# Weights converted from double by shift and masks, their exponents checked on ScalarE, with fewer conversion pieces in the attention

## The chip, the cores and the metric

The kernel runs on one core of one Trainium2 chip. The time is the device time of one execution in microseconds, as the median of three runs. The core has five engines that work in parallel, each in the order of its own program: TensorE (PE; its weight loads are shown as PEld), VectorE (DVE), ScalarE (ACT), GpSimd (POOL) and SyncE (SP), which issues nearly all DMAs here. TensorE has two clock levels, 1.2 and 2.4 GHz; the profile gives the granted clock as a share of the upper one, so 0.50 is 1.2 GHz and 1.00 is 2.4 GHz.

## The reference

The network has three parts, one behind the other. `moe_w_in`, `moe_w_out`, `moe2_w_ch1` and `moe2_w_ch2` come in as 64 bit doubles; all else is float32.

```python
# linear attention, B=4, H=8, S=768, D=48
for t in range(S):
    state = alpha[t][:, None] * state + outer(k[t], v[t])
    y[t] = q[t] @ state
# gating block: x is y with heads side by side, 768 x 384 per batch entry
h = gelu(x @ w_in)                      # w_in 384 x 1024
u, v = h[..., :512], h[..., 512:]
v = (v - mean(v)) / sqrt(var(v) + 1e-6) * g_ln
x = x + (u * (w_sg @ v + b_sg)) @ w_out # w_sg 768 x 768, w_out 512 x 384
# spectral mixing and MLP
u = x + real(fft2(x))
out = u + relu(norm(u) @ w_ch1) @ w_ch2 # w_ch1 384 x 1536, w_ch2 1536 x 384
```

## The kernel before

The order of the instructions of every engine is the order of the program text; nothing is rearranged by a scheduler. The kernel first runs the attention, then the gating block for the four batch entries, then the mixing and the MLP. Most matrix products are done three times, on a high and a low part of either operand, so weights and activations are split into `h` and `l` tiles.

**Attention.** There are 16 groups of two heads. Two scans per group on VectorE (L96, L114) form the decays, the product L115 the scaled keys, and GpSimd the scaled queries `qh` (L128). The loop runs over 32 half groups `h`, here called steps. In a step TensorE forms the scores of the next step (`sc`, L159), VectorE masks them (`att`, L164), TensorE transposes keys (`trk`, L134), ScalarE copies them to `kt` (L136), TensorE multiplies them with the values to `kp` (L146 and L147), VectorE scans `kp` into the state `z` (L151), and TensorE forms the output `y` (`pv`, L172, L173, L178), which ScalarE copies to `ys`. Scans for a group are issued two groups ahead; q and k are loaded five groups ahead.

**Weights.** The four double matrices are converted to float32 on the chip by the class `Wide`, in 62 blocks of 128 rows and 256 or 192 columns: 12 blocks of `w_in`, 8 of `w_out` (192 columns), 42 of the two MLP matrices, which are written back to memory (`w_s`) for later. A block is loaded raw as 16 bit words two blocks ahead. `first` takes exponent and upper mantissa bits out of the high word (`x`) and starts on the lower bits (`mid`); `second` sets the sign, forms the scale in `sb` and adds both parts on GpSimd (L468). In between, ScalarE changes the exponent's offset with an activation of `x` (L446, or L453). Up to the end of the attention (`on_dve`) VectorE forms `mid` with L448 and L465; later ScalarE and GpSimd do it with L451, L452, L454 and L467. Then `done` splits the result for `w_in` and `w_out` (ScalarE L392, GpSimd L395) or stores it.

`steps` is a generator that yields after each piece. While `on_dve` holds, a block is five pieces with one VectorE instruction each; later it is three pieces. Other code pulls pieces with `take`: in the attention `fill(h)` takes

```python
            if h == -1:
                take(wide, 1)
            if h >= 1:
                take(wide, 6 if h > 26 else 2)
```

`fill(29)` is called in step 30, behind the last `att`. In the gating block `gfill` takes one piece after each of the first 14 activations of a batch entry and 3 or 4 after each of the eight products with `w_sg`; `wo_ready` forces the blocks of `w_out` that the first batch entry needs.

**End.** `flag` sums up checks of the attention's scans at step 29 into `odd` (L313, L315, L316). At the end all engines load `odd` (L1167) and branch (L1168) round a general path, `attention_any` with a second `network`, which runs only where `odd` is set.

Of the kernel before, what the change touches and what calls it, by code (L numbers as in the profile page):

```python
# [317 lines left out]

def attention_any(tc, st):
# [106 lines left out]
class Wide:  # L426
    def __init__(self, nc, pool, w, const, ahead, on_dve):
        self.nc, self.pool, self.w, self.const, self.ahead, self.on_dve = nc, pool, w, const, ahead, on_dve
        self.n_done = 0
# [4 lines left out]
    def load(self, job):  # L434
        src, w, done = job
        raw = self.pool.tile([128, 4 * self.w], U16, tag="wr", name="wr", bufs=self.ahead + 2)[:, 0:4 * w]
        self.nc.sync.dma_start(raw, src)
        return dict(raw=raw, w=w, done=done, on_dve=self.on_dve, hi=raw.bitcast(I32).rearrange("p (a b) -> p a b", b=2)[:, :, 1])

    def first(self, j):  # L440
        nc, w = self.nc, j["w"]
        h16 = j["raw"].rearrange("p (a b) -> p a b", b=4)
        x, mid = j["x"], j["mid"] = self.tile("wx", I32, w, 2), self.tile("wm", F32, w, 3)
        nc.vector.tensor_scalar(out=x, in0=j["hi"], scalar1=0x7FFF0000, scalar2=None, op0=ALU.bitwise_and)
        if j["on_dve"]:
            nc.scalar.activation(x, x, AF.Relu, scale=8.0, bias=self.const)  # L446
            yield
            nc.vector.scalar_tensor_tensor(out=mid, in0=h16[:, :, 2], scalar=65536.0, in1=h16[:, :, 1], op0=ALU.mult, op1=ALU.add)  # L448
        else:
            low = j["raw"].bitcast(F32).rearrange("p (a b) -> p a b", b=2)[:, :, 0]  # L450
            nc.scalar.activation(mid, h16[:, :, 2], AF.Copy, scale=2.0 ** -20)  # L451
            nc.scalar.activation(low, h16[:, :, 1], AF.Copy, scale=2.0 ** -36)  # L452
            nc.scalar.activation(x, x, AF.Relu, scale=8.0, bias=self.const)  # L453
            nc.gpsimd.tensor_tensor(out=mid, in0=mid, in1=low, op=ALU.add)  # L454
        yield

    def second(self, j):
        nc, x, mid = self.nc, j["x"], j["mid"]
        sb = j["raw"].bitcast(I32).rearrange("p (a b) -> p a b", b=2)[:, :, 0]
# [11 lines left out]
    def steps(self, jobs):  # L471
        live = {i: self.load(jobs[i]) for i in range(self.ahead)}
        yield
        for i in range(len(jobs) + 2):
            if i - 1 in live:
                yield from self.second(live[i - 1])
            if i in live:
                yield from self.first(live[i])
# [33 lines left out]
def rows(ap, i, c, wide):  # L512
    if wide:
        ap, c = ap.bitcast(U16), slice(4 * c.start, 4 * c.stop)
    return ap[i * 128:(i + 1) * 128, c]


WJ = 256


def cols(n):
# [679 lines left out]
```

## Time and profile before

| | |
|---|---|
| median of 3 runs | 802.98 us (800.66 to 803.77) |
| the profiled execution | 801.92 us |
| its span, first to last instruction | 800.0 us |
| TensorE busy | 753.8 us (94%) |
| VectorE busy | 530.0 us (66%) |
| ScalarE busy | 292.6 us (37%) |
| GpSimd busy | 253.0 us (32%) |
| mean granted clock of TensorE | 0.962 |

Matmuls are pipelined, and their ends are modelled, so busy time of TensorE counts overlapping instructions once and says that it had work, not that it was at its peak. An engine's share over the whole span is a mean over stages that differ, so the rows below are taken by stage. The page's chain of work that ended last is empty in this profile.

### The profile page before, as it was taken

The numbers are of one execution on the slowest core, as the hardware profiler recorded it, in microseconds if no ns is written. First come the engines' busy times: TensorE is split into PE (matmuls) and PEld (weight loads), VectorE is DVE, ScalarE is ACT, GpSimd is POOL, SyncE is SP. The second block draws the span as 40 slices with busy tenths as digits, with TensorE's granted clock in tenths as the row PEclk, the third lists the DMA queues.
The fourth block names the chain that finished last, engine by engine and source line by source line (L and its number), as shares of the span: only waits on it lengthen the run. The fifth ranks groups of instructions, "written<-read, shape, count | busy, mean of one in ns | idle before, by whom it ended". The sixth has DMA issues, their size and how long they took to land.

```text
span 800.0 us, 13517 instructions
## 1 busy us (share of the span) xinstructions
PE 753.8 (94%) x5077; PEld 703.3 (88%) x5077; DVE 530.0 (66%) x1208; ACT 292.6 (37%) x719; POOL 253.0 (32%) x267
## 2 busy tenths in 40 slices
PE   6786879897999999999999999999999999999996
PEld 5575667686999998998999999999999999999996
DVE  8899999969878877876887793338433454333312
ACT  3344444436535534644532443223213322222210
POOL 2345655546655553554543464003000000000000
PEclk9789786799999999999999999999999999999999
DMA  9887788443223222221130231000000000000001
GB/s 231 208 199 180 184 201 184 113 121 108 84 79 94 79 78 61 60 76 63 36 102 1 60 99 53 18 30 2 1 31 1 30 1 1 30 17 14 31 1 34
DMA packets 43596, 59.96 MB, mean 75 GB/s; under 512 B 5056, under 2 KB 33760, under 8 KB 43520
## 3 DMA queue, kind: packets, MB, share of 16 engines
q1 hardware_dynamic: 42944, 58.73, 27.2%
q8 instruction: 42, 0.69, 0.4%
q10 hardware_dynamic: 576, 0.26, 0.1%
q14 instruction: 34, 0.28, 0.1%
HBM read 44.82 MB, written 9.44 MB: 68 GB/s over the span
## 4 chain that ended last, share of the span: by engine, by line


## 5 line engine op out<-in xcount | busy, mean ns | idle before, releaser
L970 DVE SCALAR_TENSOR_TENSOR hl<-h,hh 128x384 fp32r<-128x384 f32 x96 | 53.4, 556 | 143.4 <-ACT hh L969 143.3
L969 ACT ACTIVATE hh<-h 128x384 fp32r<-128x384 f32 x96 | 47.2, 491 | 178.1 <-PE h L423 178.1
L421 PE MATMUL h<-unh,wc 128*128 128x384 f32 x288 | 99.3, 345 | 0.0
L422 PE MATMUL h<-unl,wc 128*128 128x384 f32 x288 | 96.4, 335 | 0.1
L423 PE MATMUL a<-wc,hl 128*128 128x384 f32 x288 | 96.4, 335 | 0.0
L423 PE MATMUL h<-unh,wc 128*128 128x384 f32 x288 | 96.3, 334 | 0.0
L422 PE MATMUL a<-wc,hh 128*128 128x384 f32 x288 | 96.2, 334 | 0.0
L421 PE MATMUL a<-wc,hh 128*128 128x384 f32 x288 | 96.2, 334 | 0.0
L468 POOL TENSOR_TENSOR wm<-wx,wm 128x192 f32<-128x192 f32 (+1 forms) x62 | 60.8, 981 | 37.8 <-DVE wm L465 34.4
L423 PE MATMUL h<-wsg,vl 128*128 128x384 f32 x192 | 65.5, 341 | 2.6 <-DVE vl L642 2.6
L421 PE MATMUL h<-wsg,vh 128*128 128x384 f32 x192 | 65.1, 339 | 0.0
L422 PE MATMUL h<-wsg,vh 128*128 128x384 f32 x192 | 64.9, 338 | 0.0
L128 POOL TENSOR_TENSOR qh<-q,ak 112x768 f32<-112x768 f32 (+1 forms) x18 | 39.4, 2191 | 51.9 <-DVE ak L114 41.3
L172 PE MATMUL y<-at,v 128*64 128x128 f32 x192 | 36.6, 342 | 20.4 <-DVE at L164 20.4
L422 PEld LDWEIGHTS h<-unl,wc 128*128 128x128 f32 x288 | 54.2, 188 | 0.3 <-DVE unl L395 0.3
L423 PEld LDWEIGHTS a<-wc,hl 128*128 128x128 f32 x288 | 54.0, 188 | 0.2 <-DVE hl L970 0.2
L421 PEld LDWEIGHTS h<-unh,wc 128*128 128x128 f32 x288 | 54.1, 188 | 0.0
L467 POOL TENSOR_TENSOR wm<-wm,wr 128x192 f32<-128x192 f32 (+1 forms) x44 | 33.1, 752 | 66.3 <-DVE wr L462 66.3
L423 PEld LDWEIGHTS h<-unh,wc 128*128 128x128 f32 x288 | 54.1, 188 | 0.0
L422 PEld LDWEIGHTS a<-wc,hh 128*128 128x128 f32 x288 | 54.1, 188 | 0.0
L421 PEld LDWEIGHTS a<-wc,hh 128*128 128x128 f32 x288 | 54.0, 188 | 0.0
L172 PEld LDWEIGHTS y<-at,v 128*64 128x64 f32 x192 | 26.8, 171 | 27.3 <-DVE at L164 23.7
(207 smaller groups left out, 1929.0 us busy)
## 6 DMA issues: line engine op xcount, KB each, us to landing
ak<-in_qa SPq DMA_DIRECT2D x15, 675.1 KB, 5.6
q<-in_qa SPq DMA_DIRECT2D x15, 336.0 KB, 6.7
v<-in_v SPq DMA_DIRECT2D x16, 288.0 KB, 4.9
wr<-in_w_d SPq DMA_DIRECT2D x18, 256.0 KB, 2.7
wr<-in_w_d SPq DMA_DIRECT2D x24, 192.0 KB, 2.3
raw<-w_s SPq DMA_DIRECT2D x12, 384.0 KB, 3.2
out<-o SPq DMA_DIRECT2D x24, 192.0 KB, 1.9
wr<-in_win_d SPq DMA_DIRECT2D x12, 256.0 KB, 5.0
```

The lines of the kernel that those rows point to most:

```text
L128: P.tensor_tensor(out=flat(qhs[g % 3])[:, j], in0=d["q"][:, j], in1=d["r"][:, j], op=ALU.mult)
L172: T.matmul(y[0:HP, i, :], d["v"][:, c, 0:HP], x["at"][:, 0, j], start=i == 0, stop=c == 0, skip_group_check=True)
L421: T.matmul(out, lh, rh, start=first, stop=False)
L422: T.matmul(out, lh, rl, start=False, stop=False)
L423: T.matmul(out, ll, rh, start=False, stop=last)
L467: nc.gpsimd.tensor_tensor(out=mid, in0=mid, in1=sb.bitcast(F32), op=ALU.mult)
L468: nc.gpsimd.tensor_tensor(out=mid, in0=x.bitcast(F32), in1=mid, op=ALU.add)
L969: A.activation(hh, p, AF.Relu)
L970: V.scalar_tensor_tensor(out=hl, in0=p, scalar=0.0, in1=hh.bitcast(F32), op0=ALU.max, op1=ALU.subtract)
```

## The change

- Every block is now converted in one way, with four VectorE instructions. The high word is shifted left by 3 and masked, which keeps the low seven exponent bits and 20 mantissa bits in the places that float32 has for them; the second instruction puts sign and top exponent bit in front of them. The low part is the upper half of the low word times a scale. A block is three pieces, and they hold one, two and one VectorE instructions.
- ScalarE no longer changes the exponent. It checks instead, with three activations on the top 16 bits (absolute value twice, then Relu with a running sum), that the exponent fits; the sum goes to a column of `wodd`. The old way with more bits is kept in the general path (`general`).
- `fill` takes 2 pieces a step until 12 blocks are done, then none until step 26, then 4.
- After the network, `odd_weights` adds all sums of `wodd` and the old `odd`, by a product on TensorE and a reduction on VectorE, into `odd`.
- `wconst` and `wodd` take the place of `bias`; the scratch for DMA descriptors is set to 8192 bytes.

```diff
+def odd_weights(tc, st):
+    nc = tc.nc
+    with tc.tile_pool(name="odd_p", bufs=1, space=PSUM, reuse_waits="tile") as ps, tc.tile_pool(name="odd_s", bufs=1, side="right", reuse_waits="tile") as sb:
+        one, p, s = sb.tile([128, 2], F32, name="oddo"), ps.tile([2, NWJ + 1], F32, name="oddp"), sb.tile([2, 1], F32, name="odds")
+        nc.vector.memset(one, 1.0)
+        nc.vector.tensor_copy(st["wodd"][0:1, NWJ:], st["odd"])
+        nc.tensor.matmul(p, one, st["wodd"], start=True, stop=True)
+        nc.vector.tensor_reduce(out=s, in_=p, axis=mybir.AxisListType.X, op=ALU.add)
+        nc.vector.tensor_scalar(out=st["odd"], in0=s[0:1], scalar1=0.0, scalar2=None, op0=ALU.not_equal)
...
-    def first(self, j):
-        nc, w = self.nc, j["w"]
-        h16 = j["raw"].rearrange("p (a b) -> p a b", b=4)
-        x, mid = j["x"], j["mid"] = self.tile("wx", I32, w, 2), self.tile("wm", F32, w, 3)
-        nc.vector.tensor_scalar(out=x, in0=j["hi"], scalar1=0x7FFF0000, scalar2=None, op0=ALU.bitwise_and)
-        if j["on_dve"]:
-            nc.scalar.activation(x, x, AF.Relu, scale=8.0, bias=self.const)
-            yield
-            nc.vector.scalar_tensor_tensor(out=mid, in0=h16[:, :, 2], scalar=65536.0, in1=h16[:, :, 1], op0=ALU.mult, op1=ALU.add)
+    def check(self, j, n):
+        A, t = self.nc.scalar, self.tile("wk", F32, j["w"], 1)
+        A.activation(t, j["top"], AF.Abs, bias=self.const[:, 1:2])
+        A.activation(t, t, AF.Abs, bias=self.const[:, 2:3])
+        A.activation(t, t, AF.Relu, bias=self.const[:, 3:4], accum_out=self.odd[:, n:n + 1])
+
+    def first(self, j, n):
+        V, hi = self.nc.vector, j["hi"]
+        x, mid = j["x"], j["mid"] = self.tile("wx", I32, j["w"], 2), self.tile("wm", F32, j["w"], 3)
+        if self.general:
...
         else:
-            low = j["raw"].bitcast(F32).rearrange("p (a b) -> p a b", b=2)[:, :, 0]
-            nc.scalar.activation(mid, h16[:, :, 2], AF.Copy, scale=2.0 ** -20)
-            nc.scalar.activation(low, h16[:, :, 1], AF.Copy, scale=2.0 ** -36)
-            nc.scalar.activation(x, x, AF.Relu, scale=8.0, bias=self.const)
-            nc.gpsimd.tensor_tensor(out=mid, in0=mid, in1=low, op=ALU.add)
+            self.check(j, n)
+            V.tensor_scalar(out=x, in0=hi, scalar1=3, scalar2=0x3FFFFFF8, op0=ALU.logical_shift_left, op1=ALU.bitwise_and)
         yield
...
-        nc.vector.scalar_tensor_tensor(out=x, in0=j["hi"], scalar=-2 ** 31, in1=x, op0=ALU.bitwise_and, op1=ALU.bitwise_or)
+        V, x, mid, hi = self.nc.vector, j["x"], j["mid"], j["hi"]
+        V.scalar_tensor_tensor(out=x, in0=hi, scalar=-2 ** 31 if self.general else -2 ** 30, in1=x, op0=ALU.bitwise_and, op1=ALU.bitwise_or)
         yield
-        nc.vector.tensor_scalar(out=sb, in0=x, scalar1=-2 ** 23, scalar2=None, op0=ALU.bitwise_and)
-        if j["on_dve"]:
-            yield
-            nc.vector.scalar_tensor_tensor(out=mid, in0=mid, scalar=2.0 ** -36, in1=sb.bitcast(F32), op0=ALU.mult, op1=ALU.mult)
-        else:
-            nc.gpsimd.tensor_tensor(out=mid, in0=mid, in1=sb.bitcast(F32), op=ALU.mult)
-        nc.gpsimd.tensor_tensor(out=mid, in0=x.bitcast(F32), in1=mid, op=ALU.add)
+        V.tensor_scalar(out=hi, in0=x, scalar1=-2 ** 23, scalar2=None, op0=ALU.bitwise_and)
+        V.scalar_tensor_tensor(out=mid, in0=mid if self.general else j["low"], scalar=2.0 ** -36, in1=hi.bitcast(F32), op0=ALU.mult, op1=ALU.mult)
+        self.nc.gpsimd.tensor_tensor(out=mid, in0=x.bitcast(F32), in1=mid, op=ALU.add)
         yield
...
-    st["bias"] = per.tile([128, 1], F32, name="bias")
-    nc.vector.memset(st["bias"], -896.0 * 2 ** 23)
+    st["wconst"] = per.tile([128, 4], F32, name="wconst")
+    st["wodd"] = per.tile([128, NWJ + 1], F32, name="wodd")
+    for i, v in enumerate((-896.0 * 2 ** 23, -32768.0, -16384.0, -2030.5)):
+        nc.vector.memset(st["wconst"][:, i:i + 1], v)
+    nc.vector.memset(st["wodd"], 0.0)
...
-                take(wide, 6 if h > 26 else 2)
+                take(wide, 4 if h > 26 else 2 if st["converted"]() < 12 else 0)
...
     network(tc, st, "", front)
+    odd_weights(tc, st)
...
-    nc = _bacc.Bacc("TRN2", target_bir_lowering=False, num_devices=1)
+    nc = _bacc.Bacc("TRN2", target_bir_lowering=False, num_devices=1, dynamic_dma_scratch_size=8192)
```

## Rows read from the trace of the kernel before

**Rows 1.** Windows by stage: us, busy us (instructions) per engine, granted clock, DMA.

```profile
0.00:166.90 166.90, 134.11 (x1499) 104.42 (x1499) 154.69 (x237) 66.53 (x194) 77.70 (x53) 0.84 0.76 182
166.90:205.00 38.10, 32.80 (x155) 28.18 (x154) 31.56 (x71) 21.62 (x54) 21.60 (x26) 0.97 0.42 120
240.00:430.00 190.00, 189.98 (x1064) 181.71 (x1063) 149.71 (x360) 90.40 (x222) 92.08 (x124) 1.00 0.23 68
```

**Rows 2.** Timeline of VectorE: start us, us, engine, line and operation.

```profile
33.41 0.95 DVE L164 TENSOR_TENSOR at<-sp,mask 128x768 f32<-128x768 f32 x1
...
76.04 2.98 DVE L448 SCALAR_TENSOR_TENSOR wm<-wr 128x256 f32<-128x256 uint16 x1
...
148.72 0.95 DVE L164 TENSOR_TENSOR at<-sp,mask 128x768 f32<-128x768 f32 x1
...
163.94 0.96 DVE L164 TENSOR_TENSOR at<-sp,mask 128x768 f32<-128x768 f32 x1
```

**Rows 3.** Waits from 0 to 230 us: who for whom, us in total, times, longest.

```profile
ACT wx L446 <- DVE wx L444: 32.2, 18, 3.8
...
PE y L172 <- DVE at L164: 20.4, 15, 3.0
...
DVE z L151 <- PE kp L147: 4.5, 4, 1.5
...
PE h L423 <- DVE vl L642: 2.6, 3, 1.1
...
PE h L421 <- ACT ut L649: 1.5, 2, 1.0
...
PE h L421 <- ACT vt L630: 1.1, 1, 1.1
```

**Rows 4.** Windows of 4 us in the attention, TensorE alone, columns as in rows 1.

```profile
112.00:116.00 4.00, 3.96 (x61) 1.00 1.13 223
128.00:132.00 4.00, 4.00 (x34) 0.50 0.99 267
```

**Rows 5.** Groups by line and form, VectorE, 0 to 205 us: busy us, mean ns | idle before.

```profile
L448 DVE SCALAR_TENSOR_TENSOR wm<-wr 128x256 f32<-128x256 uint16 x12 | 7.7, 645 | 0.0
...
L460 DVE SCALAR_TENSOR_TENSOR wx<-wr,wx 128x256 int32<-128x256 int32 x12 | 7.7, 642 | 0.2 <-ACT wx L446 0.2
...
L462 DVE TENSOR_SCALAR wr<-wx 128x256 int32<-128x256 int32 x12 | 5.4, 449 | 0.2
...
L465 DVE SCALAR_TENSOR_TENSOR wm<-wm,wr 128x256 f32<-128x256 f32 x12 | 5.1, 425 | 0.2
...
L444 DVE TENSOR_SCALAR wx<-wr 128x256 int32<-128x256 int32 x13 | 3.8, 289 | 0.0
```

**Rows 6.** Groups by line and form, ScalarE, 0 to 205 us.

```profile
L446 ACT ACTIVATE wx<-wx,bias 128x256 int32<-128x256 int32 x12 | 6.1, 509 | 22.1 <-DVE wx L444 22.1
...
L120 ACT ACTIVATION_READ_ACCUMULATOR junk<-ak,rng 112x1 f32 x17 | 3.3, 193 | 0.0
...
L218 ACT ACT_TABLE_LOAD x1 | 1.3, 1283 | 2.6 <-issue 2.6
```

**Rows 7.** Groups by line and form, GpSimd, 0 to 205 and 205 to 405 us.

```profile
L468 POOL TENSOR_TENSOR wm<-wx,wm 128x256 f32<-128x256 f32 x12 | 20.3, 1694 | 22.3 <-DVE wm L465 22.3
...
L467 POOL TENSOR_TENSOR wm<-wm,wr 128x256 f32<-128x256 f32 x18 | 14.7, 816 | 25.1 <-DVE wr L462 25.1
```

**Rows 8.** Timeline and single lines: duration ns min/median/max, first and last start.

```profile
L315 DVE TENSOR_REDUCE fs<-fp x1: 155/155/155, 163.7 to 163.7; 2x1 f32<-2x34 f32 x1
...
792.58 0.61 DVE L980 SCALAR_TENSOR_TENSOR o<-a,my,x 128x384 f32<-128x384 f32 x1
...
L1167 SPq TENSOR_LOAD <-odd x1: 558/558/558, 794.5 to 794.5; - x1
...
L1168 SPq EVENT_SEMAPHORE  x8: 17/17/17, 798.1 to 798.7; - x8
...
L1168 PEldq COMPARE_BRANCH  x1: 3657/3657/3657, 791.2 to 791.2; - x1
```

More of the change, by code (lines that the diff above doesn't have):

```diff
@@ L426, with __init__ @@
 class Wide:
-    def __init__(self, nc, pool, w, const, ahead, on_dve):
-        self.nc, self.pool, self.w, self.const, self.ahead, self.on_dve = nc, pool, w, const, ahead, on_dve
+    def __init__(self, nc, pool, w, const, ahead, general, odd):
+        self.nc, self.pool, self.w, self.const, self.ahead, self.general, self.odd = nc, pool, w, const, ahead, general, odd
         self.n_done = 0
@@ L477, in steps @@
             if i in live:
-                yield from self.first(live[i])
+                yield from self.first(live[i], i)
             if i + self.ahead < len(jobs):
@@ L509, in to_hl, with rows, wide_rows @@
     return lambda r: split(nc, dst[0], dst[1], r, eh, el)
-def rows(ap, i, c, wide):
-    if wide:
-        ap, c = ap.bitcast(U16), slice(4 * c.start, 4 * c.stop)
+def rows(ap, i, c):
     return ap[i * 128:(i + 1) * 128, c]
+def wide_rows(ap, i, c):
+    return ap.bitcast(U16)[i * 128:(i + 1) * 128, 4 * c.start:4 * c.stop]
 WJ = 256
+NWJ = 2 * KD * DH // WJ + 2 * KH + 12 * KD // 2 + 24
 def cols(n):
@@ L530, in win_jobs @@
                 c = slice(h * DH + c.start, h * DH + c.stop)
-                js.append((rows(st["win_d"], i, c, True), c.stop - c.start, to_hl(nc, [w[:, i, c] for w in st["win"]], nc.scalar, nc.gpsimd)))
+                js.append((wide_rows(st["win_d"], i, c), c.stop - c.start, to_hl(nc, [w[:, i, c] for w in st["win"]], nc.scalar, nc.gpsimd)))
     return js
@@ L537, in put @@
         return lambda r: split(nc, st["wsg"][0][:, i, c], st["wsg"][1][:, i, c], r, nc.scalar, nc.vector if i in (0, 2) else nc.gpsimd)
-    return [(rows(st["wsg_d"], i, c, False), HT, put(i, c)) for i in range(NT) for c in (slice(0, HT), slice(HT, S))]
+    return [(rows(st["wsg_d"], i, c), HT, put(i, c)) for i in range(NT) for c in (slice(0, HT), slice(HT, S))]
 def wo_jobs(nc, st):
@@ L544, in wo_jobs @@
         for c in (slice(0, 192), slice(192, 384)):
-            js.append((rows(st["wo_d"], i, c, True), 192, to_hl(nc, [w[:, i, c] for w in st["wo"]], nc.scalar, nc.gpsimd)))
+            js.append((wide_rows(st["wo_d"], i, c), 192, to_hl(nc, [w[:, i, c] for w in st["wo"]], nc.scalar, nc.gpsimd)))
     return js
@@ L557, in spill_jobs @@
                 c = slice(c, c + w)
-                js.append((rows(st[d], i, c, True), w, put(n, i, c)))
+                js.append((wide_rows(st[d], i, c), w, put(n, i, c)))
     return js
@@ L1054, in network @@
     st["xl"] = w1l.tile([128, NT, KD, CH], F32R, name="xl")
-    wd = Wide(nc, pool(in_u, "wide", "left"), WJ, st["bias"], 2, True)
+    wd = Wide(nc, pool(in_u, "wide", "left"), WJ, st["wconst"], 2, tag != "", st["wodd"])
     F = {}
```

18 lines of the change are left out of this document (11 added, 7 removed).

## The prediction

> **What bounds the kernel now.** The stages come first [rows 1]: the attention fills the first 166.9 us, the gating block follows in four batches, and from 240 us TensorE is busy in 189.98 of 190.00 us. A change to VectorE, ScalarE or GpSimd gains nothing there as long as VectorE, at 149.7 of 190, stays below full. Before that TensorE idles 32.8 us (166.90 - 134.11) in the attention and 5.3 us (38.10 - 32.80) in the first batch, to 205 us. So the gain has to be found before 205 us.
>
> In the attention VectorE is busy 154.7 of 166.9 us. The attention has 32 steps (`h`), each with one masking product, L164. From step 3 at 33.41 us to step 27 at 148.72 us that is 115.3/24 = 4.80 us a step; the last four take (163.94 - 148.72)/4 = 3.81 us [rows 2], since the scans of later groups have ended by then. The waits say the same [rows 3]: TensorE stands 20.4 us for L164, VectorE only 4.5 us for TensorE's `kp`. But TensorE is not far behind. Its 1,499 instructions [rows 1] are 47 a step. Where it ran without a gap it did 61 in 4 us at a granted clock of 1.00 and 34 at 0.50 [rows 4]: 3.1 us a step at 2.4 GHz, 5.5 us at 1.2 GHz. At the upper level VectorE sets the pace, at the lower one TensorE would.
>
> In the first batch the waits of TensorE are for `vl` of VectorE, 2.6 us, and for `ut` and `vt` of ScalarE, 1.5 and 1.1 us [rows 3]: together 5.2 of the 5.3 us.
>
> **The change in the attention.** A weight block passed through five VectorE instructions; by mean durations of the 256 wide form [rows 5] that is 0.289 + 0.645 + 0.642 + 0.449 + 0.425 = 2.45 us, or 0.490 an instruction. L448 is dropped and the other four remain, with other operands but as many elements: 1.805 us a block, 0.451 an instruction. The trace has no shift followed by a mask, nor the last product with a 16 bit input. From below I bound the first by L444, from above by L460 (both of 256 elements), and take L444, which is the same class of instruction with one scalar; the second by L465 and L448, and take L465.
>
> The steps decide how much of this arrives. Before, `fill` takes 2 pieces a step from step 1 to 26, each with one VectorE instruction: 52 instructions, ten blocks and the first two pieces of the eleventh, 10 x 2.45 + 0.93 = 25.4 us. Now a block is three pieces with four instructions (the last pieces hold two). Block 0 needs one piece and each further round three, and twelve blocks are counted as done only in the 42nd piece: 2 a step from step 1 to 21, none from 22 to 26. That is 14 blocks, 14 x 1.805 = 25.3 us with the two narrow ones at the wide price. So the VectorE time in the stretch where VectorE is the bound stays as it was, 25.4 to 25.3: fewer instructions a block are spent on more blocks. They are also bunched: +2.67 x 0.451 - 2 x 0.490 = +0.22 us a step for 21 steps, +4.7 us, then -0.98 us for five, -4.9 us. In steps 27 and 28, the last before the last L164, it was 12 instructions and is now 8 pieces with 10.7: 4.8 against 5.9 us, at most 1.1 us less, but there the steps are short already and VectorE has spare time. I take 0 for the whole, from -4.5 us (all waits for `kp` gone) up to +7.7 (rival two).
>
> ScalarE: L446, 0.509 us, is replaced by three activations with a bias operand and a reading of the sum. Priced as L446 and the read of the accumulator [rows 6] that is 3 x 0.509 + 0.193 = 1.72 us, +1.2 us a block, 17 us over 14 blocks, with ScalarE busy 66.5 of 166.9 us. What waits behind them are the copies of `kt` and `ys`. On the other hand L446 stood 32.2 us for L444 with these copies behind it [rows 3]; the new checks read only the loaded block, so this wait goes and no new one comes. I take nothing for both together. The cover is ScalarE's idle time; without it, each block would delay a copy by 1.7 us. Constants and sums are cleared by five small memsets before the first scan, which waits for its load anyhow: nothing. Loads on SyncE's queue are the same, earlier by some steps; two of them a step at most, and VectorE waits for none after the start: nothing. The smaller scratch for descriptors touches no issue seen here: nothing.
>
> GpSimd keeps one addition a block, L468, at 1.69 us [rows 7], but for 14 blocks instead of 10 by step 26. That is +6.8 us of GpSimd in a stretch where the two disturb each other: one L448 lasts 2.98 us [rows 2], while the other eleven come to (7.7 - 2.98)/11 = 0.43 us [rows 5]. L448 and L460 are each 0.22 us above L465, which has as many elements: 12 x 0.44 = 5.3 us beside 20.3 us of L468, or 0.26 us for each us of GpSimd. For 6.8 us that is +1.8 us; but the surplus of L460 stands in the price of 1.805 us already, and L448's is dropped with it. I add nothing and keep +1.8 us for the range.
>
> The Trainium skill (SBUF — State Buffer, Who interferes with whom) states that a VectorE instruction with two SBUF inputs and a GpSimd instruction that reads SBUF fully block each other. The trace agrees for L448, with its 2.98 us, and for L164, which has one input in PSUM and is 0.95 or 0.96 us in the three rows shown. What that rule could do at its hardest is rival four.
>
> **The first batch, 166.9 to 205 us.** Once `fill` has ended, 14 pieces fall here; they held 14 VectorE instructions and now hold 14 x 4/3 = 18.7, which is +2.1 us at 0.451. Against it, L467 of 0.82 us a block and L454, which has the same form, leave GpSimd [rows 7]. The output weights are converted by then but for the last block, so their casts and splits leave this stretch too. ScalarE no longer stands for L444 ahead of `vt`, 2.6 us of the 5.2 us of waits depend on it, and I count half: -1.3 us. The VectorE half (`vl`) I leave. Bounds: -5.3 (no idle left) to +2.1.
>
> **The rest.** Here a block had three VectorE instructions and now has four; the fourth is of L465's kind, 0.43 us. ScalarE exchanges three activations for three and a reading of 0.19 us; GpSimd loses two of its three additions. Three more batches have 14 blocks each: +6 us of VectorE a batch of some 61 us, +18 us on 149.7 of 190 us. TensorE stays the bound: nothing. If VectorE's cover were gone it would be these 18 us.
>
> **The end.** `odd` is now found after the last output: a copy on VectorE, a product on TensorE, a sum, a test; then five engines load it, four of which had done so before. The last L980 ends at 792.58 + 0.61 = 793.19 us; the sum of the same flag in the attention, L315, is 0.16 us [rows 8]; four such steps and three handovers that I estimate at the same to twice as long are 1.1 to 1.6 us: `odd` at 794.3 to 794.8, while SyncE loaded it at 794.5. TensorE's branch after it takes 3.66 us from 791.2 us; now it would begin about half a us after the flag, behind the load, and end at 798.5 to 799.0; SyncE's last waits run at 798.7. So 0 to +0.7, I take +0.3 us.
>
> **Sum.** 0 - 1.3 + 0.3 = -1.0 us. The profiled execution took 801.92 us (span 800.0 and 1.9 around it), 1.1 below the median 802.98. From the first that is 800.9, from the median 802.0. I forecast 801.0. Half a per cent, 4 us, is about what can be told from no change.
>
> **Rivals.** *One, faster: late copies were the trouble.* ScalarE freed from L446's waits delivers `kt` in time, VectorE's 4.5 us of waits for `kp` go, and so do TensorE's 2.6 us for ScalarE in the first batch: -7.1 + 0.3 gives 795.1. For it speaks the sum of 32.2 us; against it, that a TensorE at 0.50 makes `kp` late too, whatever ScalarE does. Faster by over 4 us from a bit more than half of it.
>
> *Two, slower: the saving is not collected.* Steps 1 to 21 pay 4.7 us; in 22 to 26 TensorE runs at 1.2 GHz and needs 5.5 us a step against 4.80. Instead of -4.9 us they give +0.6 x 5 = +3.0. That is +7.7 - 1.0: 808.6 us. Two of such five steps keep it within 4 us; with four or more at that level it is slower. For it speaks that the trace has stretches at 0.50 as well as at 1.00 [rows 4]; against it, that at 1.00 TensorE idles less when VectorE is faster, and the mean over the attention is 0.84 [rows 1].
>
> *Three, slower: absolute value needs another table.* Before, one table load of 1.28 us [rows 6] serves all functions. If each check between two of the gating block's activations needed two loads, 14 x 2 x 1.28 = 36 us a batch would come on ScalarE, which has 100 us free in 190; the first batch, where TensorE waits for it, pays for 4.7 blocks 12 us: 813. The Trainium skill (ScalarE: Activation LUTs, Table sets: the hidden batching unit) says that the absolute value stands in every set, which speaks against; no row of before shows it.
>
> *Four, slower: GpSimd holds VectorE up for all of its added 6.8 us.* Then 801.0 + 6.8 = 807.8 us. Against it: in the attention 77.7 us of GpSimd [rows 1] cost VectorE far less than that. It decides from 0.9 us of stall for each us, 6.0 us in all.
>
> **Chances.** The forecast, within 4 us of 803: 0.47. Rival one, whole or in part: 0.34. Rival two 0.12, three 0.03, four 0.04. So faster 0.34, same 0.47, slower 0.19. The range must take in most of rival one and part of two: 793 to 808 us; that of the forecast alone is 799 to 804.
>
> **What would show it.** Right: L448 and ScalarE's waits for L444 gone; four instructions a block at some 1.8 us; L164 of step 22 later by 3 to 5 us than before, then steps under 4 us; TensorE's start on the gating block within 2 us of 166.9; its idle time to 205 us under 4.5 us; no second table load; 240 us onward full. Wrong: an attention that ends 4 us earlier or later, a granted clock near 0.50 through steps 22 to 26, idle time of TensorE after 240 us, or an end more than 1 us longer after the last L980.

## The result and the profile after

The changed kernel took 806.87 us (median of 7 executions, 805.57 to 808.17) against 800.66 us (7 executions, 797.98 to 803.77) for the kernel before on the same chip: ratio 1.0075, 95% interval 1.0051 to 1.0099. It is slower by some 0.75%; the forecast was 801.0 us, no change. On a second chip the ratio was 1.0064 (run e5 below). A ratio leaves out executions that the chip disturbed, so it can differ from the quotient of the medians beside it. Run e4's profiled execution took 812.37 us, 6 us over the median of its run, so its trace is used only where that is said.

The profiled execution of the changed kernel is the fastest of its seven, 805.57 us with a span of 803.4 us, against 801.92 and 800.0 before. So the traces account for 3.65 of the 6.2 us between the medians: 3.40 in the span and 0.25 around it. The rest is spread over executions that were not profiled.

First the stages, as in [rows 1]: us, then busy us and instructions of TensorE, its weight loads, VectorE, ScalarE and GpSimd, granted clock, DMA share, GB/s.

```profile
0.00:166.90 166.90, 133.55 (x1448) 103.47 (x1450) 155.39 (x235) 86.17 (x251) 87.07 (x59) 0.81 0.75 185
166.90:205.00 38.10, 33.34 (x186) 28.85 (x185) 28.42 (x71) 26.21 (x66) 17.17 (x21) 0.91 0.55 150
240.00:430.00 190.00, 190.00 (x1066) 182.35 (x1065) 147.24 (x369) 95.09 (x228) 35.02 (x50) 1.00 0.20 58
```

TensorE is still full from 240 us on, and VectorE is full before 166.9 us. The steps of the attention, by the masking product L164 of steps 3, 22, 27 and 31, as in [rows 2] (steps are counted from 0):

```profile
32.59 0.95 DVE L164 TENSOR_TENSOR at<-sp,mask 128x768 f32<-128x768 f32 x1
...
134.37 0.94 DVE L164 TENSOR_TENSOR at<-sp,mask 128x768 f32<-128x768 f32 x1
...
154.08 0.95 DVE L164 TENSOR_TENSOR at<-sp,mask 128x768 f32<-128x768 f32 x1
...
167.74 0.96 DVE L164 TENSOR_TENSOR at<-sp,mask 128x768 f32<-128x768 f32 x1 [0.20 <-PE sp L159]
```

[Rows 2] lack step 22 of the kernel before, which is this row:

```profile
124.65 0.94 DVE L164 TENSOR_TENSOR at<-sp,mask 128x768 f32<-128x768 f32 x1
```

Steps 3 to 22 went from 91.24 us (124.65 - 33.41) to 101.78 us, +10.54. Steps 22 to 27 went from 24.07 to 19.71 us, -4.36, and steps 27 to 31 from 15.22 to 13.66 us, -1.56. Step 3 came 0.82 us earlier. So the L164 of step 31 is 3.80 us later.

The start of each batch entry on TensorE tells the rest. Timeline of TensorE, after:

```profile
171.89 0.50 PE L432 MATMUL h<-win,xh 128*128 128x512 f32 x1
...
241.30 0.39 PE L432 MATMUL h<-win,xh 128*128 128x512 f32 x1
...
303.58 0.39 PE L432 MATMUL h<-win,xh 128*128 128x512 f32 x1
```

and before:

```profile
166.86 0.50 PE L421 MATMUL h<-win,xh 128*128 128x512 f32 x1
...
237.56 0.39 PE L421 MATMUL h<-win,xh 128*128 128x512 f32 x1
...
300.80 0.39 PE L421 MATMUL h<-win,xh 128*128 128x512 f32 x1
```

The gating block starts 5.03 us later, the second batch 3.74, the third 2.78. From there on the distance stays: the last output begins at 794.30 us and at 791.52 before, again 2.78. The end adds 0.62.

Where steps 3 to 22 went: the window of those steps in both kernels, then the groups of VectorE and GpSimd by line (busy us, mean ns, idle before). Before:

```profile
33.41:124.65 91.24, 72.28 (x875) 56.86 (x876) 89.85 (x124) 38.64 (x115) 48.47 (x30) 0.82 0.80 192
...
L96 DVE TENSOR_TENSOR_SCAN sf<-ak,d1s 112x768 f32<-112x768 f32 x9 | 16.3, 1807 | 0.0
L115 DVE TENSOR_TENSOR sf<-ak,sf 112x768 f32<-112x768 f32 x10 | 10.8, 1076 | 0.0
...
L468 POOL TENSOR_TENSOR wm<-wx,wm 128x256 f32<-128x256 f32 x8 | 14.2, 1772 | 18.0 <-DVE wm L465 18.0
L395 POOL TENSOR_TENSOR xl<-x,xh 128x384 fp32r<-128x384 f32 x6 | 6.9, 1149 | 0.0
L395 POOL TENSOR_TENSOR win<-wm,win 128x256 fp32r<-128x256 f32 x6 | 5.4, 894 | 3.6 <-ACT win L392 3.6
```

After:

```profile
32.59:134.37 101.78, 81.65 (x875) 63.52 (x876) 99.03 (x137) 56.65 (x166) 64.68 (x40) 0.72 0.74 184
...
L96 DVE TENSOR_TENSOR_SCAN sf<-ak,d1s 112x768 f32<-112x768 f32 x9 | 17.9, 1990 | 0.0
L115 DVE TENSOR_TENSOR sf<-ak,sf 112x768 f32<-112x768 f32 x10 | 13.3, 1333 | 0.0
...
L478 POOL TENSOR_TENSOR wm<-wx,wm 128x256 f32<-128x256 f32 (+1 forms) x13 | 19.1, 1471 | 21.3 <-DVE wm L477 21.3
L406 POOL TENSOR_TENSOR xl<-x,xh 128x384 fp32r<-128x384 f32 x6 | 11.6, 1933 | 0.1
L406 POOL TENSOR_TENSOR win<-wm,win 128x256 fp32r<-128x256 f32 x11 | 11.3, 1028 | 14.6 <-ACT win L403 14.6
```

VectorE has 13 instructions more and 9.2 us more busy time (99.03 - 89.85); its idle time grew from 1.39 to 2.75 us. The 13 are conversions: their groups in this view sum to 20.0 us before and 24.1 us after, +4.1. The other 5 us come from instructions that both kernels have in the same number: L115 and L96 alone, nineteen instructions, take 4.1 us longer, and nine of L98 1.2 us. The granted clock in these steps is 0.72 where it was 0.82, but that does not make them longer: VectorE idles only 2.75 us of them, and the same kernel once more (e5) took 101.67 us at 0.76. GpSimd beside them has 16.2 us more (64.68 - 48.47): five more additions (+4.9 us), five more splits of `win` (+5.9), the six splits of `x`, unchanged in number, at 1933 in place of 1149 ns (+4.7), and 0.8 us of the ten scaled queries.

The waits from 0 to 230 us, as in [rows 3]: who for whom, us, times, longest.

```profile
PE y L172 <- DVE at L164: 18.2, 15, 4.1
...
PE h L432 <- ACT ut L662: 3.3, 2, 3.0
...
ACT wk L454 <- DMA wr<-in_wo_d: 3.3, 2, 2.5
...
PE kp L146 <- ACT kt L136: 1.9, 1, 1.9
DVE z L151 <- PE kp L147: 1.9, 2, 1.1
...
PE h L432 <- ACT vt L643: 1.4, 1, 1.4
...
PE h L434 <- DVE vl L655: 0.5, 1, 0.5
```

ScalarE's 32.2 us behind L444 are gone. In their place it stands at the first check, L454, for a load of `w_out`, once for 2.5 us, with the copy `kt` behind it: TensorE then waits 1.9 us for `kt`, in step 30. The waits for `vl`, `ut` and `vt` sum to 5.2 us as before, moved from VectorE to ScalarE.

The new instructions on VectorE, 0 to 205 us by line and form, against [rows 5], and two of ScalarE's, against [rows 6]:

```profile
L474 DVE SCALAR_TENSOR_TENSOR wx<-wr,wx 128x256 int32<-128x256 int32 x16 | 10.8, 673 | 0.2
L477 DVE SCALAR_TENSOR_TENSOR wm<-wr 128x256 f32<-128x256 uint16 x16 | 8.9, 553 | 1.7 <-DVE wr L476 0.5
L476 DVE TENSOR_SCALAR wr<-wx 128x256 int32<-128x256 int32 x16 | 6.8, 424 | 0.4
L469 DVE TENSOR_SCALAR wx<-wr 128x256 int32<-128x256 int32 x17 | 5.4, 319 | 2.8 <-DMA wr<-in_w_d 2.8
...
L454 ACT ACTIVATE wk<-wr,wconst 128x256 f32<-128x256 uint16 x17 | 8.9, 523 | 4.3 <-DMA wr<-in_w_d 2.4 <-DMA wr<-in_win_d 1.9
...
L456 ACT ACTIVATION_READ_ACCUMULATOR wk<-wk,wconst 128x1 f32 x24 | 4.5, 186 | 0.0
```

A block costs VectorE 0.673 + 0.553 + 0.424 + 0.319 = 1.97 us, where 1.805 was reckoned; the low product is the one that is dearer (0.553 for 0.425). The end, against [rows 8]:

```profile
794.30 1.67 DVE L993 SCALAR_TENSOR_TENSOR o<-a,my,x 128x384 f32<-128x384 f32 x3 [1.00 <-PE a L434]
...
796.63 0.14 DVE L327 TENSOR_SCALAR odd<-odds 1x1 int32<-1x1 f32 x1
...
L1184 SPq TENSOR_LOAD <-odd x1: 622/622/622, 796.8 to 796.8; - x1
...
L1185 PEldq COMPARE_BRANCH  x1: 3374/3374/3374, 797.5 to 797.5; - x1
```

`odd` stands 0.8 us after the last output (796.77 - 795.97), is loaded, and TensorE's branch runs from 797.5 to 800.9 us. From the last output to the end of the span it is 7.43 us against 6.81.

### The profile page after: what moved, and what is told of

Its sections match the earlier page's. It is cut to its first block, busy times and chain, and to the rows that moved or that the text cites. A ratio compares the mean times of both kernels' runs of the same rounds, so it can differ in the third digit from the quotient of the medians.

```text
span 803.4 us, 13559 instructions
## 1 busy us (share of the span) xinstructions
PE 756.7 (94%) x5079; PEld 706.2 (88%) x5079; DVE 531.6 (66%) x1242; ACT 330.0 (41%) x817; POOL 186.4 (23%) x179
## 4 chain that ended last, share of the span: by engine, by line
PE 73%; DVE 17%; DMA 3%; issue 2%; ACT 2%; SPq 1%; POOL 1%; DVEq 0%; POOLq 0%; ACTq 0%
PE h L432 14%; PE h L433 14%; PE h L434 14%; PE a L434 8%; PE a L432 8%; PE a L433 8%; DVE sf L96 3%; DVE ak L114 2%; PE h L835 2%; DVE at L164 2%; DVE wx L474 2%; DVE sf L115 1%; DMA ak<-in_qa 1%; PE h L836 1%; PE h L891 1%
## 5 line engine op out<-in xcount | busy, mean ns | idle before, releaser
L478 POOL TENSOR_TENSOR wm<-wx,wm 128x192 f32<-128x192 f32 (+1 forms) x62 | 54.4, 878 | 175.9 <-DVE wm L477 167.4
L686 ACT CAST gh<-t 128x384 fp32r<-128x384 f32 x32 | 16.4, 514 | 60.1 <-DVE t L683 58.7
```

The lines of the kernel that those rows point to most:

```text
L478: self.nc.gpsimd.tensor_tensor(out=mid, in0=x.bitcast(F32), in1=mid, op=ALU.add)
L686: A.copy(gh, t1)
```

## The experiments

All runs at one glance. A ratio is against the kernel before on the same chip, with its 95% interval; the other columns are read from the traces of profiled executions.

| run | median us | ratio | steps 3 to 22, us | gating block starts, us |
|---|---|---|---|---|
| before | 800.66 to 804.28 | 1 | 91.24 | 166.86 |
| changed kernel | 806.87 | 1.0075 [1.0051, 1.0099] | 101.78 | 171.89 |
| e5 changed kernel again | 808.18 | 1.0064 [1.0038, 1.0089] | 101.67 | 172.19 |
| e1 even pace | 810.93 | 1.010 [1.0063, 1.0136] | 99.43 | 169.84 |
| e2 block pace of before | 802.48 | 0.9978 [0.9947, 1.001] | 91.16 | 167.47 |
| e3 addition on 8 columns | 803.44 | 1.0014 [0.9978, 1.005] | 95.76 | 167.52 |
| e4 no checks | 806.34 | 1.0007 [0.9972, 1.0043] | 100.87 | 178.64 |
| e13 no checks again | 804.18 | 1.0019 [0.9987, 1.0052] | 101.72 | 169.08 |
| e7 before, dense pace | 808.32 | 1.0055 [1.0038, 1.0072] | 103.36 | 171.60 |
| e8 early test | 807.14, one time | | 102.40 | 174.26 |
| e9 addition on VectorE | 809.2 | 1.008 [1.0052, 1.0109] | 100.57 | 170.30 |
| e12 addition twice | 812.92, one time | | 106.15 | 179.47 |
| e6 shift and or | 797.7 | 0.9934 [0.9908, 0.996] | 91.38 | 160.60 |
| e10 the same, early test | 798.32 | 0.9958 [0.9935, 0.998] | 94.41 | 162.90 |
| e11 the same, block pace of before | 788.71 | 0.9836 [0.9801, 0.9871] | 84.52 | 153.02 |
| e14 e11 without checks | 789.1 | 0.9826 [0.9789, 0.9864] | 86.92 | 158.95 |
| e15 e11, one piece a step | 790.45 | 0.9839 [0.9801, 0.9877] | 88.15 | 161.46 |

Up to the gating block the changed kernel, e5 and e8 are the same program. Their three traces differ by 0.7 us in steps 3 to 22 and by 2.4 us in the start of the gating block: smaller differences than these can't be told from one trace.

The change does three things at once: other instructions, another pace in the attention, and checks on ScalarE. The runs take them apart.

### The pace

**e1_even** spreads the pieces of the changed kernel over all steps.

```diff
-                take(wide, 4 if h > 26 else 2 if st["converted"]() < 12 else 0)
+                take(wide, 4 if h > 28 else 2 if h % 5 else 1)
```

> The changed kernel with its pieces spread evenly over the attention: 2 a step but 1 in every fifth, 51 pieces before the last L164 instead of 50, and 4 a step at the end. Theory A (VectorE bound up to step 27, and its work grows with the blocks converted beside the scans, by the instructions themselves and by stalls behind GpSimd): the sum of work before the last L164 is the same, so the time is the changed kernel's within 2 us and L164 of step 31 starts at 166 to 170 us. Theory B (the bunching costs the time, since what steps 1 to 21 pay is not given back in 22 to 26): 3 to 5 us less than the changed kernel.

It took 810.93 us, ratio 1.010. The L164 of step 31 stands at 166.91 us, where theory A had it; the 3 to 5 us that theory B hoped for are not there. The gating block starts 2 us earlier than in the changed kernel, but steps 22 to 27 take 23.66 us where they took 19.71. So it is not the bunching as such that costs.

**e2_pace** gives a step as many blocks as before: 1.2 pieces of three to a block where it was 2 of five.

```diff
-                take(wide, 4 if h > 26 else 2 if st["converted"]() < 12 else 0)
+                take(wide, 4 if h > 26 else 1 if h % 5 else 2)
```

> The changed kernel with the block pace of before: 31 pieces (10.3 blocks) in steps 1 to 26 instead of 42, then 4 a step. Theory A: 11 pieces fewer are about 15 VectorE instructions of 0.50 us and some 12 us of GpSimd at a third of a us of stall each, 7 to 11 us earlier at step 27, most of it kept to the last L164; the first batch has to convert more of the output weights and gives back up to 4 us. So 3 to 9 us below the changed kernel, and below the kernel before. Theory C (the checks on ScalarE or the later flag make it slower, not the pace): it stays within 2 us of the changed kernel.

802.48 us, ratio 0.9978, an interval that takes in 1. Steps 3 to 22 are back at 91.16 us, and the loss is gone; theory C falls. Yet 31 conversion instructions with 12.0 us stand there where before had 38 with 20.0 us, and the steps are no shorter: VectorE idles 4.6 us against 1.4, and its other instructions, which are the same in both kernels, take 3.8 us more, though GpSimd has as many additions (8) and splits of `win` (6) as before. First the two kinds of conversion that showed stalls before, then one of them in e2 (the other, L477, has 425 ns too), and L115, which had 1076 ns:

```profile
L448 DVE SCALAR_TENSOR_TENSOR wm<-wr 128x256 f32<-128x256 uint16 x7 | 5.7, 810 | 0.0
L460 DVE SCALAR_TENSOR_TENSOR wx<-wr,wx 128x256 int32<-128x256 int32 x8 | 5.2, 651 | 0.0
```

```profile
L474 DVE SCALAR_TENSOR_TENSOR wx<-wr,wx 128x256 int32<-128x256 int32 x8 | 3.4, 425 | 0.0
L115 DVE TENSOR_TENSOR sf<-ak,sf 112x768 f32<-112x768 f32 x10 | 12.8, 1275 | 0.0
```

Over 425 ns, L448 and L460 had 4.5 us together (7 x 0.385 + 8 x 0.226). In e2 the conversions show none of it, and L115, L96 and L98 have gained 2.0, 1.6 and 0.9 us (L114 lost 0.8). The stalls did not go with L448; they show on other instructions.

**e7_before_dense** is the opposite test: the old conversion, unchanged, at a denser pace.

```diff
-                take(wide, 6 if h > 26 else 2)
+                take(wide, 6 if h > 26 else 3 if h < 22 else 0)
```

> The kernel before with three pieces a step from step 1 to 21 and none from 22 to 26, 63 pieces in place of 52: the order of the change without its instructions. Theory A (it is the denser conversion beside the scans that costs): the L164 of step 22 at 132 to 136 us in place of 124.65, steps 22 to 27 in 20 us, the gating block 2 to 5 us later than before, ratio 1.002 to 1.007. Theory B (it is the new instructions or the checks): 21 x 0.49 us of VectorE more by step 22 and the same less after it, the gating block within 1 us of before and the ratio within 0.002 of 1.

808.32 us, ratio 1.0055 [1.0038, 1.0072]: the denser pace, without one new instruction, loses about as much as the whole change. Window of its steps 3 to 22:

```profile
32.26:135.62 103.36, 82.43 (x893) 64.58 (x893) 101.72 (x143) 41.75 (x123) 63.31 (x38) 0.73 0.74 182
```

GpSimd has 63.31 us in it, as in the changed kernel (64.68), and VectorE is full. But the loss is made up otherwise: nineteen conversions more (+10.7 us) are most of it, and VectorE's other instructions grew by 2.2 us, not 5.0. Its steps 22 to 27 take 20.71 us; what they and the last four give back (3.4 and 2.7 us) is half of what steps 3 to 22 cost (12.1 us).

### GpSimd beside the scans

**e5_after_again** is the changed kernel, unedited, as a control for the three runs beside it.

> The changed kernel as it is, on the chip on which the next three run, since single executions of one kernel differ by some 4 us and the first comparison was made on another chip. If its loss belongs to the kernel it is again 1.005 to 1.010; if it belonged to that chip the ratio is 1.00.

1.0064 [1.0038, 1.0089], and a trace that agrees with the first within 0.3 us in both columns of the table. The loss belongs to the kernel.

**e3_thin_add** leaves the addition on GpSimd out for all but 8 of a block's columns.

```diff
-        self.nc.gpsimd.tensor_tensor(out=mid, in0=x.bitcast(F32), in1=mid, op=ALU.add)
+        self.nc.gpsimd.tensor_tensor(out=mid[:, 0:8], in0=x[:, 0:8].bitcast(F32), in1=mid[:, 0:8], op=ALU.add)
```

> The changed kernel with the addition L478 on GpSimd done for 8 columns of a block only; the other columns lack the upper part. All else, the splits on GpSimd too, is as in the changed kernel. Theory A with stalls: some 19 us of GpSimd leave steps 3 to 22, and at 0.35 us of stall for each us the last L164 comes 5 to 8 us earlier; L115, L98 and the weight instructions come near their shortest durations. If the stalls are not the cause but only the number of VectorE instructions, the change is under 2 us.

803.44 us, ratio 1.0014. Steps 3 to 22 with the same 137 instructions of VectorE:

```profile
32.24:128.00 95.76, 81.66 (x893) 64.08 (x893) 92.58 (x137) 56.97 (x167) 56.61 (x40) 0.73 0.80 197
...
L115 DVE TENSOR_TENSOR sf<-ak,sf 112x768 f32<-112x768 f32 x10 | 11.5, 1155 | 0.0
L478 POOL TENSOR_TENSOR wm<-wx,wm 128x8 f32<-128x8 f32 x13 | 12.5, 963 | 18.8 <-DVE wm L477 18.8
```

6.0 us less than in the changed kernel, for 8.1 us less of GpSimd. Thirteen additions of 8 columns still show 963 ns each, so the cut took away a third of the additions' time and no more. VectorE's instructions other than conversions are back at 77.8 us, where they were before the change (77.7), though all eleven splits of `win` are still there.

**e12_double_add** goes the other way.

```diff
+        self.nc.gpsimd.tensor_tensor(out=self.tile("wq", F32, j["w"], 1), in0=x.bitcast(F32), in1=mid, op=ALU.add)
         self.nc.gpsimd.tensor_tensor(out=mid, in0=x.bitcast(F32), in1=mid, op=ALU.add)
```

> Every addition of a block on GpSimd runs twice, the first time into a buffer that nobody reads. Theory A (an addition on GpSimd costs VectorE about 0.4 us): 12 more of 1.4 us from step 3 to 22, +17 us of GpSimd, the stretch of L96 and L115 up by 4 to 5 us, the L164 of step 22 at 138 to 140 us. Theory B (the stalls come from the splits and from the pace alone): within 1 us of 134.4.

```profile
33.66:139.81 106.15, 85.05 (x875) 66.26 (x876) 103.41 (x138) 56.85 (x166) 79.17 (x52) 0.69 0.70 177
...
L115 DVE TENSOR_TENSOR sf<-ak,sf 112x768 f32<-112x768 f32 x10 | 14.0, 1404 | 0.0
```

Step 22 at 139.81 us, as theory A said, though L96 and L115 together hardly grew (31.2 to 31.4 us): the time fell on L107, L98 and the conversions. Thirteen additions more are 19.9 us of GpSimd; the whole of GpSimd grew by 14.5 us (79.17 - 64.68), since one scaled query fell out of the window and the splits of `x` were shorter. The steps take 4.4 us more: 0.34 us for each addition, 0.22 for each us of additions. In e3 it was 6.0 us for 6.6 us of additions (19.1 to 12.5), 0.9 for each. So there is no one rate.

**e9_add_on_vector** moves the addition to VectorE.

```diff
-        self.nc.gpsimd.tensor_tensor(out=mid, in0=x.bitcast(F32), in1=mid, op=ALU.add)
+        V.tensor_tensor(out=mid, in0=x.bitcast(F32), in1=mid, op=ALU.add)
```

> The changed kernel with the last addition of a block on VectorE in place of GpSimd: 13 instructions of about 0.44 us more on VectorE from step 3 to 22, +5.7 us, and 19 us less on GpSimd. Theory A (each addition on GpSimd costs the scans beside it about 0.4 us, as with the 8 columns): the stretch of L96 and L115 falls by 4 to 5 us, the L164 of step 22 stays within 2 us of 134.4, ratio 1.003 to 1.008. Theory B (GpSimd costs more than it does in the table, since its splits and the copy of the query are late too): the L164 of step 22 2 us or more earlier, ratio at most 1.001. Theory C (GpSimd's additions cost nothing): step 22 at 139 us or later, ratio over 1.010.

Ratio 1.008, steps 3 to 22 at 100.57 us, step 22 at 133.55: theory A. L115 falls to 1155 ns and L96 from 1990 to 1749, and thirteen additions of 472 ns on VectorE eat that up. An addition costs VectorE about the same on either engine.

**e6_or_low_bits** has no addition.

```diff
...
+        if not self.general:
+            V.scalar_tensor_tensor(out=mid.bitcast(I32), in0=j["lo"], scalar=29, in1=x, op0=ALU.logical_shift_right, op1=ALU.bitwise_or)
+            yield
+            return
         V.tensor_scalar(out=hi, in0=x, scalar1=-2 ** 23, scalar2=None, op0=ALU.bitwise_and)
```

> The top three bits of the low half are set into the mantissa by one shift and or (they are cut off where the change rounds): three VectorE instructions a block in place of four, and no addition on GpSimd. Theory A (the loss is VectorE's and GpSimd's added work beside the scans of steps 1 to 21): 14 instructions of 0.45 us less, 6 us, and 19 us of GpSimd less with some 4 us of L96's and L115's stalls; the L164 of step 22 at 124 to 127 us in place of 134, the gating block from 164 to 167, ratio 0.990 to 0.998. Theory B (TensorE is nearly as far behind as VectorE, so that less work only turns into waits for kp): VectorE idles 5 us or more in steps 3 to 31 and the gating block starts at 169 or later, ratio 1.002 to 1.008.

797.7 us, ratio 0.9934 [0.9908, 0.996], at the pace of the changed kernel:

```profile
33.07:124.45 91.38, 74.94 (x889) 58.86 (x891) 89.52 (x124) 56.32 (x167) 38.56 (x27) 0.80 0.81 204
```

10.4 us less in steps 3 to 22 with 13 VectorE instructions less and 26 us less of GpSimd. VectorE idles 1.9 us there, so theory B falls; the gating block starts at 160.60 us, earlier than theory A had it.

Steps 3 to 22 of these runs, by sums of the groups of each view, number and us (instructions overlap a little, so the sums exceed the busy time):

| run | conversions on VectorE | its other instructions, us | additions on GpSimd | splits of `win` |
|---|---|---|---|---|
| before | 38, 20.0 | 77.7 | 8, 14.2 | 6, 5.4 |
| changed kernel | 51, 24.1 | 82.8 | 13, 19.1 | 11, 11.3 |
| e5 changed kernel again | 51, 24.0 | 82.8 | 13, 19.1 | 11, 11.4 |
| e2 block pace of before | 31, 12.0 | 81.5 | 8, 16.9 | 6, 5.4 |
| e7 before, dense pace | 57, 30.7 | 79.9 | 12, 20.9 | 10, 11.6 |
| e3 addition on 8 columns | 51, 22.4 | 77.8 | 13, 12.5 | 11, 11.4 |
| e6 shift and or | 38, 21.1 | 76.2 | 0 | 11, 10.2 |
| e13 no checks | 51, 23.2 | 82.6 | 13, 19.1 | 11, 9.2 |

The other instructions are the same in every row. Their 5.0 us in the changed kernel hang on the additions: they go where these are cut (e3) or gone (e6); 3.8 of them stay where the splits are as few as before (e2), and 4.9 where the checks are gone (e13).

### The checks on ScalarE

**e4_no_check** and **e13_no_check_again** drop the call of `check`, **e14_best_no_check** does the same in the kernel e11 below; the exponents are then not checked.

```diff
-            self.check(j, n)
```

> The changed kernel without the three activations and the reading that check the exponents; the sums stay zero, the flag is formed as before. Theory A: ScalarE is not on the path in the attention; within 1.5 us of the changed kernel. Theory C (ScalarE's added 17 us delay the copies of kt and ys and the activations of the first batch): 3 to 6 us less, with the waits of TensorE for ut and vt in the first batch (3.3 and 1.4 us) gone.

> The changed kernel without its exponent checks once more (no check is computed, so the general path can't be chosen by it). In the first comparison its ratio was 1.0007 [0.9972, 1.0043], between no loss and the whole one. Theory A (ScalarE's checks are off the path: 100.9 us against 101.8 in steps 3 to 22): ratio 1.003 to 1.008, the L164 of step 22 within 1.5 us of 134.4. Theory B (the checks delay kt, ys, vt and ut and make some 0.5% of the loss): ratio 0.998 to 1.002, and the gating block or its first two batches at least 3 us earlier than in the changed kernel.

> The fastest kernel so far (low bits by shift and or, the test early, the block pace of before) without the exponent checks. Theory A: within 0.3% of that kernel, ratio 0.981 to 0.987. Theory B: 0.4 to 0.6% below it, 0.977 to 0.980.

Ratios 1.0007 and 1.0019, where the changed kernel has 1.0075 and 1.0064; the intervals of e13 and e5 overlap. Steps 3 to 22 are the same with or without (101.72 and 101.78 us): there the checks cost nothing. In these traces the difference lies after step 27. From the L164 of step 27 to the start of the gating block, first the changed kernel, then e13:

```profile
154.08:171.89 17.81, 14.62 (x197) 11.33 (x196) 14.86 (x31) 11.37 (x36) 7.15 (x9) 0.90 0.51 126
```

```profile
154.33:169.08 14.75, 13.07 (x197) 10.26 (x195) 14.04 (x28) 5.47 (x18) 6.31 (x8) 1.00 0.55 140
```

3.1 us; e5 and e8, with checks, take 17.92 and 17.80. Without checks, ScalarE doesn't stand for the load of `w_out`, TensorE doesn't wait 1.9 us for `kt`, and its granted clock stays at 1.00; in the changed kernel the last 4.15 us of this stretch, from step 31's L164 on, run at 0.67, where the kernel before needs 2.92 us at 1.00 for the same instructions. That the wait and the lower clock belong together is an argument from their order, not shown. Nor does the 3.1 us hold for every execution: in e4's trace, also without checks, the same stretch takes 20.20 us at a granted clock of 0.70, with TensorE busy throughout. In e14 the cut gains nothing (0.9826 against 0.9836, the intervals overlap): the fastest kernel has ScalarE's wait of 2.5 us too, but in its trace no wait of TensorE for `kt` stands behind it. So the checks take, by the ratios, about half a per cent of the changed kernel's time and nothing measurable of the fastest kernel's; where that half per cent arises rests on one trace.

### The end, and a kernel that beats both

**e8_early_odd** tests the flag right after the last conversion, in the gating block, in a PSUM bank that is free there.

```diff
...
+        if tag == "":
+            odd_weights(tc, st)
         in_u.close()
...
```

> The sum over the exponent checks, its test and the copy of the flag run after the last conversion in the gating block and not after the last output. If these steps are on the path at the end, the time from the end of the last L993 (here of the same instruction under its own line) to the end of the span is 6.8 us as before the change, and 7.4 us if something else, the branch of five engines, makes the end longer. The total tells nothing of 0.6 us.

The last output and SyncE's last waits in it:

```profile
796.99 1.67 DVE L992 SCALAR_TENSOR_TENSOR o<-a,my,x 128x384 f32<-128x384 f32 x3 [1.00 <-PE a L433]
...
L1186 SPq EVENT_SEMAPHORE  x8: 17/17/17, 803.1 to 803.6; - x8
```

From the last output (798.66) to the end of the span (805.0) it is 6.3 us: 1.1 less than in the changed kernel and 0.5 less than before. That agrees with a late test on the path at the end, by one execution of each (7.5 us in e5).

**e10_or_early** joins e6 and e8, and **e11_or_early_pace** adds the pace of e2.

> The shift and or of the low bits, and the test of the exponents right after the last conversion. In the kernel with the or alone 10.5 us lay between the end of the last output on VectorE (785.4) and the end of the span, 3.1 us more than in the changed kernel; in the one with the early test 6.3. If the late test is what costs, 6.3 to 6.8 us here and ratio 0.986 to 0.991; if the 3.1 us come from elsewhere, 9 us or more and ratio 0.991 to 0.994.

> The same with the pace in blocks of the kernel before: 31 pieces from step 1 to 26 and four a step after that, 51 in place of 62. Theory A (a block beside the scans costs its instructions and the stalls by GpSimd's splits): 12 instructions of 0.5 us less by step 22, its L164 at 116 to 120 us in place of 124.45, steps 22 to 27 as in the kernel with that pace, 22 us, the gating block at 155 to 158, ratio 0.983 to 0.988. Theory B (TensorE is the next bound, with the 4.6 us of idle time that this pace had): the gating block at 160 or later and the ratio as that of the other of these two.

e10 took 798.32 us, ratio 0.9958; its interval overlaps that of e6, so the early test shows no gain in the total. Its end takes 8.3 us and that of e6 10.6. In both, SyncE stands a second time in the last semaphore line, which the changed kernel doesn't show. Neither expectation holds, and the cause of these 2 to 3 us is open.

e11 took 788.71 us, ratio 0.9836 [0.9801, 0.9871]: 1.6% faster than the kernel before. The steps 3 to 22 of its profiled execution, the fastest of its six with 784.92 us:

```profile
31.01:115.53 84.52, 74.97 (x894) 58.92 (x893) 81.55 (x109) 47.33 (x139) 37.19 (x22) 0.79 0.86 209
```

VectorE has 15 instructions less than before and GpSimd 11 us less; its L164 of step 22 stands at 115.53 us, and the gating block starts at 153.02 us, 2 us earlier than theory A hoped for. Its end is 6.5 us.

**e15_lean_pace** takes one piece in every step up to 26.

> The fastest kernel so far with one piece a step from step 1 to 26 and four after that, 46 pieces in place of 51. Theory A (what is converted beside the scans costs): 3 to 4 pieces less by step 22, 1.5 to 2.5 us, the gating block at 150.5 to 152 us, and the ratio 0.001 to 0.003 below that of the kernel with 51. Theory B (TensorE or the conversions needed by the gating block take over): the same ratio or more, with waits of TensorE for wo or for vl in the first batch.

790.45 us, ratio 0.9839 [0.9801, 0.9877]: no gain over e11. Its profiled execution, at 796.73 us, is the slowest of its six; in that trace VectorE idles 9.7 us in steps 3 to 22 where e11 has 3.0 and e14, at the pace of e11, 5.6. The trace of e11 is its fastest execution, so the two compare badly; by the ratio fewer conversions gain nothing more. That is theory B, though the expected waits of TensorE for `wo` are not there.

## Why the prediction was wrong

- **What bounds the kernel** held: nothing moved after the second batch, and all of the loss arose before 171.9 us, in the steps where VectorE is the bound.
- **The step that failed** is the one on GpSimd in the attention: "I add nothing and keep +1.8 us for the range." It gave the added GpSimd time a price of nothing, because the stalls that L448 had shown would be "dropped with it". Measured in steps 3 to 22: +4.9 us of additions, and +5.0 us on the VectorE instructions that both kernels have. The credit was wrong: e2, without L448 and with as many additions and splits as before, already has 3.8 of these 5.0 us; the stalls of L448 and L460 moved to L115, L96 and L98, which VectorE can't drop. The other 1.3 us came with the denser pace. Nor does the rate of 0.26 us for each us of additions carry over: the runs give 0.9 (e3) and 0.22 (e12), and why they differ is open.
- **The bunching** was reckoned right. +4.7 us of conversions up to step 21 was forecast, +4.1 measured in steps 3 to 22; -4.9 us for the five empty steps, -4.36 measured. Their sum is nothing, as said. What made steps 3 to 22 dearer by 10.54 us is these 4.1, the stalls of 5.0 and 1.4 us more of idle time. That a block takes 1.97 us and not 1.805 is in the 4.1. The L164 of step 22 came 9.7 us late where 3 to 5 was forecast, and that was the row to watch.
- **ScalarE, "this wait goes and no new one comes"**: the wait for L444 went, and a new one came, for a load, since a check reads the raw block itself and blocks are taken faster than before. It is 2.5 us once, with the cover gone in step 30. Against e13 the stretch behind step 27 lost 3.1 us; that this is the wait is not shown.
- **The first batch**: -1.3 forecast, -1.29 measured by the starts of the batches. That was luck: the waits named sum to 5.2 us as before, and what gained the time is open. The second batch gave back 0.96 us that I hadn't seen; no wait names it, and TensorE is full in it in both kernels.
- **The rest** at nothing and **the end** at +0.3 (0 to +0.7): nothing after 303 us, +0.62 at the end. The summing took 0.8 us in place of 1.1 to 1.6, but the branches start behind it.
- **The sum**: -1.0 forecast, +3.65 in the profiled executions. Attention 0 forecast, +5.03 measured, is the error of 4.65 us; the other terms miss by -0.4 together. That 806.87 us lies in the range of 793 to 808 is owed to the room left for rivals, not to the sum.
- **The rivals**: rival one fell, since VectorE's waits for `kp` did go (4.5 to 1.9 us) and brought nothing visible. Rival two comes near the total with 808.6, by the wrong way: the saving in steps 22 to 26 was collected, at a granted clock of 0.86 there. Rival three fell: no second table load. Rival four, at a chance of 0.04, was the nearest in kind and in size: 807.8, by 6.8 us of stalls where 5.0 were measured. Its rule of a us for each us does not hold in general, though: e12 shows 0.22, and most of the 5.0 us are stalls that had stood on L448 and L460.

The Trainium skill (SBUF — State Buffer, Who interferes with whom) says that VectorE with two SBUF inputs and a GpSimd instruction that reads SBUF contend for shared ports, by an exclusive lock. These traces bear it out in whom it hits: L115 and L96, with two such inputs, grew from 1076 to 1333 and from 1807 to 1990 ns, and L164, with one input in PSUM, stayed between 0.93 and 0.98 us in every run. L98, with a single SBUF input, grew too, from 288 to 423 ns, which two inputs don't explain. In how much it costs the runs differ: e3 got back 0.9 us for each us of additions, e12 lost 0.22.

What stays open: what gained the 1.29 us of the first batch and the 0.96 us of the second, the second wait of SyncE at the end of e6 and e10, and at what rate additions on GpSimd cost VectorE time.

## What to carry to other kernels

Count everything that a finished block sets off, on every engine, when it is made faster per block but more blocks are pulled into the bounding stage: here the saving of a fifth of VectorE's work per block (2.45 to 1.97 us) was spent on more blocks beside the scans, and their additions came along. Nor is a stall saved with the instruction that shows it: while the other engine's work is still there, it can fall on the next instruction. A saving per item is worth its price only where the items per step stay the same; here the change at the old pace lost nothing (e2), and with the addition gone and the test early it is worth 1.6% (e11). And where an engine in order gets work that reads a transfer directly, its other duties wait for that transfer, as the copy `kt` did behind 2.5 us.

## What the runs showed of the hardware that was not expected

- An addition on GpSimd over 8 columns took 963 ns in the crowded steps, one over 256 columns 1416 ns: there a thirty-second of the work saves a third of the time.
- Thirteen additions more on GpSimd (+19.9 us) cost the steps 4.4 us (e12); a cut of 6.6 us of them gave back 6.0 us (e3). With the addition on VectorE itself (472 ns) steps 3 to 22 took 1.2 us less than with it on GpSimd (1471 ns).
- Stalls moved from the instructions that were dropped to others: L448 and L460 had shown 4.5 us of them, and without L448 L115, L96 and L98 took 4.5 us more, at the same number of additions (e2).
